# The seam between attention and experts: another order for the last period, earlier token splits, a one-step router sum, ScalarE scaling

## Chip, cores and metric

The kernel runs on one core of one Trainium2 chip. The metric is device time in microseconds; the median of the runs is compared. All times below are of one core.

## What is computed

Block-causal attention over 8 batches x 8 heads x 576 rows x 64 columns in float32 (a query block of 64 sees all key blocks up to its own). The heads are laid side by side into 4608 tokens of 512 numbers, which go through a two-level mixture of experts: a group softmax (4 groups) and an expert softmax inside the chosen group (4 experts), the best of each taken; then two layers of the one chosen expert, scaled by both weights.

```
scores = where(block_i >= block_j, q @ k.T / 8, -1e9)
x = softmax(scores) @ v                     # -> (4608, 512)
g = argmax(x @ w_group);  e = argmax(x @ w_expert[g])
out = p_g * p_e * (relu(x @ w1[g, e]) @ w2[g, e])
```

## The kernel before

The program is one list of instructions per engine, in an order that the kernel writes out by hand. Each engine works through its own list in order. TensorE, VectorE (DVE in the rows), ScalarE (ACT), GpSimd (POOL) and SyncE (SP, which issues most DMAs) are kept in step by semaphores.

**Attention.** 32 pairs of heads (4 pairs per batch) go through a software pipeline of periods. `ORDER` is the order of steps in one period: `S8@1` is the scores of row block 8 of the pair one period back, `D` the row maxima (VectorE), `E` the exponentials (ScalarE), `T` the transposes of the probabilities, `t` their evacuation to SBUF, `V` the values, `v` their evacuation, `K`, `k`, `j`, `h`, `l` the preparation of queries and keys. Four periods make a batch, and the router's steps of a finished batch ride in the same list: `R` reciprocals of the softmax sums, `X` transposes of the attention output to token rows, their scaling and their store to DRAM (`xd`), `L`/`n` router logits, `Y` their small transposes, `M` the sum of the logits over heads, `G0` and `G1` the two picks (group, expert), `G2` the prefix counts, `G4` the rank matmuls, `G3` the places, `Z` five scatters of token ids into the table `tab` (GpSimd). `LAST` names the router steps that are left over.

**PSUM.** During the attention one pool of four buffers of two banks rotates (`wide`). `experts()` closes it and opens the pools of the experts: `ps_h` (first layer), `ps_y` (two output banks), `ps_m0` and `ps_m1`. Some of the new tiles lie over buffers that must be read out first.

**Experts.** Slot "e" is the early expert: 512 tokens of the fullest expert over the first six batches, found by `early`, gathered (`xge`, four gathers of 128 rows) before the last two batches are done. So expert work can start while the last router results are still being made. The other slots run after `final` has made the row table (`rowi`) of all batches; their ids are read and their tokens gathered (`xg`). Weights arrive as `raw` pieces and are split into two float32r parts: `wh` by a ScalarE cast, `wl` by a VectorE subtraction (`piece`, two halves per unit); so are the tokens (`xt`) and the activations (`g1`: `hi` by ScalarE's relu, `lf` by VectorE). A unit `g1` (first layer) or `g2` (second) of slot "e" is 12 matmuls of 512 columns. `plan` writes the order of the units and a due time for each weight piece; `run` goes through it, and `hooks` hang the last batch's router steps behind units by number. In slot "e" the order was g1 0, g1 1, g2 0, g1 2, g2 1, and so on; `FREE` is the unit from which weights and gathers of the routed experts may be issued.

**The seam.** Order of issue before: the last period (scores, values of pair 30, transposes of pair 31), the left-over steps of batch 6, `R` of batch 7, two chunks of early tokens split (`xts`), the first weight pieces, the values of pair 31, the other two chunks, weights, unit g1 0, the logits `L` of batch 7, unit g1 1, `X0`, `Y`, `M`, `X1`, `X2`, the new PSUM pools, `G0`, `G1`, then the units with `G2`, `G4`, `G3`, `Z` and `final` behind units 2 to 4.

## Time and profile before

| what | value |
|---|---|
| median of 3 runs | 837.87 us (837.8 to 838.12) |
| profiled execution: time, span | 836.7 us, 835.0 us |
| mean granted TensorE clock | 0.991 |
| TensorE matmuls busy | 795.5 us (95%) |
| VectorE / ScalarE / GpSimd busy | 529.3 / 504.6 / 265.9 us |

A row of the timeline gives the start in microseconds from the span's start, the busy time of the group of like instructions, engine and line, what is written from what, the count, and in brackets how long the engine had been idle and what ended that. "issue" stands where the profile names no releaser. The granted clock is 1.00 at 2.4 GHz and 0.50 at 1.2 GHz.

### The profile page before, as it was taken

The page shows a single profiled execution, that of the slowest core. Times are in us where ns is not written, and L with a number is a line of the kernel's source. Part 1 is how long each engine was busy: PE and PEld are TensorE (multiplying, and loading weights), DVE is VectorE, ACT ScalarE, POOL GpSimd, SP SyncE. Part 2 cuts the span into 40 slices and gives each one's busy share as a digit, 9 for nine tenths or more (in the row PEclk, how much of TensorE's full clock was granted, in tenths as well). Part 3 has the DMA queues.
Part 4 walks back from the last instruction along what each step waited for, and adds up shares of the span by engine and source line. Part 5 has one row for each costly group of instructions (what it writes and reads, how often), then busy time and mean ns, then how long its engine had stood idle before and what let it go on. Part 6 is the DMA issues. An engine that isn't in the chain of part 4 may idle for free.

```text
span 835.0 us, 20289 instructions
## 1 busy us (share of the span) xinstructions
PE 795.5 (95%) x7649; PEld 649.7 (78%) x7649; DVE 529.3 (63%) x1102; ACT 504.6 (60%) x1273; POOL 265.9 (32%) x444
## 2 busy tenths in 40 slices
PE   8899999999999999879999999999999999999996
PEld 4677777777777777657888888888988989888885
DVE  4566989898989898668353544554444655655552
ACT  4899999999999998742342433433344445545541
POOL 3563344444444345443232211221221221131101
PEclk9899999999999999999999999999999999999999
DMA  7466473626363633641555736645544666575471
GB/s 153 114 185 181 109 157 78 155 71 150 83 152 78 145 84 90 198 153 36 177 166 162 236 117 205 201 133 192 197 145 148 203 207 191 179 237 177 151 236 39
DMA packets 182258, 126.67 MB, mean 152 GB/s; under 512 B 124902, under 2 KB 156214, under 8 KB 182160
## 3 DMA queue, kind: packets, MB, share of 16 engines
q1 hardware_dynamic: 173072, 100.73, 43.4%
q0 software_dynamic: 9088, 24.64, 8.6%
q8 instruction: 61, 1.00, 0.6%
q14 instruction: 37, 0.30, 0.1%
HBM read 100.88 MB, written 24.59 MB: 150 GB/s over the span
## 4 chain that ended last, share of the span: by engine, by line
PE 54%; DVE 1%; issue 0%; POOLq 0%; ACT 0%; ACTq 0%
PE y L1002 20%; PE h L957 19%; PE y L1007 5%; PE h L952 4%; PE ye L1002 2%; PE xp L925 2%; PE he L957 2%; POOLq L1293 0%; DVE gsc L712 0%; DVE gdd L710 0%; DVE goh L714 0%; DVE pre L742 0%; PE spill L612 0%; ACT ys L1024 0%; DVE sel L724 0%
## 5 line engine op out<-in xcount | busy, mean ns | idle before, releaser
L242 ACT ACTIVATE pb<-s,nm 128x512 f32<-128x512 f32 (+4 forms) x288 | 156.7, 556 | 31.3 <-DVE nm L230 26.7
L957 PE MATMUL h<-xt,wh 128*128 128x264 f32 (+6 forms) x704 | 155.3, 312 | 0.0
L909 DVE TENSOR_TENSOR wl<-raw,wh 128x512 fp32r<-128x512 f32 x192 | 123.4, 685 | 11.2 <-ACT wh L908 10.6
L230 DVE TENSOR_REDUCE nm<-s 128x2 f32<-128x1024 f32 (+4 forms) x160 | 122.9, 801 | 11.1 <-PE s L225 5.8
L957 PEld LDWEIGHTS h<-xt,wh 128*128 128x128 f32 x704 | 119.3, 188 | 9.1
L908 ACT CAST wh<-raw 128x512 fp32r<-128x512 f32 x192 | 108.8, 620 | 2.0 <-DMA raw<-in_moe_w_dram 1.7
L957 PE MATMUL h<-xt,wl 128*128 128x264 f32 (+6 forms) x352 | 109.3, 311 | 0.0
L1002 PE MATMUL y<-wh,hring 128*128 128x512 f32 x306 | 107.2, 401 | 0.0
L221 PE MATMUL s<-qk 64*128 64x512 f32 (+3 forms) x768 | 90.8, 351 | 12.6 <-ACT pb L242 7.3
L275 ACT COPY pt<-tp 128x1024 f32<-128x1024 f32 (+4 forms) x160 | 100.8, 747 | 0.5 <-PE tp L150 0.5
L1031 POOL DMA_INDIRECT out_dram<-ys,ids x40 | 41.2, 1029 | 183.4 <-DVE ys L1027 170.0
L970 ACT ACTIVATE hring<-h 128x288 fp32r<-128x288 f32 (+7 forms) x62 | 28.9, 466 | 114.0 <-PE h L957 55.3
L974 DVE SCALAR_TENSOR_TENSOR hring<-h,hring 128x32 fp32r<-128x32 f32 (+7 forms) x112 | 35.7, 357 | 97.5 <-ACT hring L970 89.2
L304 PE MATMUL o<-pt,vb 128*64 128x320 f32 (+4 forms) x896 | 93.9, 360 | 1.1 <-issue 1.1
L187 POOL CAST qk<-nf 128x640 fp32r<-128x640 f32 (+1 forms) x63 | 43.0, 694 | 150.8 <-ACT nf L275 140.4
L304 PEld LDWEIGHTS o<-pt,vb 128*64 128x64 f32 x896 | 59.6, 137 | 35.9 <-issue 5.1
L221 PEld LDWEIGHTS s<-qk 64*128 64x128 f32 x768 | 58.9, 190 | 24.8 <-issue 11.2
L872 POOL DMA_INDIRECT xg<-xd,ids x40 | 42.0, 1049 | 105.7 <-DMA ids<-tab 55.5
L150 PE MATMUL tp<-ident,pb 64*128 64x64 f32 x1600 | 65.5, 227 | 7.6 <-ACT pb L242 6.8
L150 PEld LDWEIGHTS tp<-ident,pb 64*128 64x128 f32 x1600 | 58.1, 141 | 14.3 <-ACT pb L242 8.0
L957 PEld LDWEIGHTS h<-xt,wl 128*128 128x128 f32 x352 | 66.2, 188 | 1.2
L1002 PEld LDWEIGHTS y<-wh,hring 128*128 128x128 f32 x306 | 57.6, 188 | 11.8
(236 smaller groups left out, 1396.5 us busy)
## 6 DMA issues: line engine op xcount, KB each, us to landing
raw<-in_moe_w_dram SPq DMA_DIRECT2D x96, 512.0 KB
natk<-in_k_dram SPq DMA_DIRECT2D x32, 256.0 KB
natq<-in_q_dram SPq DMA_DIRECT2D x32, 256.0 KB
vb<-in_v_dram SPq DMA_DIRECT2D x64, 128.0 KB
wh<-in_moe_w_dram SPq DMA_DIRECT2D x16, 512.0 KB
xd<-xns SPq DMA_DIRECT2D x14, 512.0 KB
tab<-fill POOLq DMA_DIRECT2D x10, 512.0 KB
rawe<-in_moe_w_dram SPq DMA_DIRECT2D x8, 512.0 KB
```

Source lines behind the costliest of these rows:

```text
L150: self.nc.tensor.transpose(out=out[:, z], in_=src[r], identity=self.c["ident"][r, r])
L187: (eng or self.side(("h", n))).tensor_copy(r["qk"][:, 0, o], r["nf"][:, o])
L221: nc.tensor.matmul(st[:, z, :], lhsT=t[p, hq, S + P * u:S + P * u + P], rhs=t[p, hk, 0:w], start=x == 0, stop=False)
L230: self.nc.vector.tensor_reduce(out=o, in_=r["s", u], op=ALU.max, axis=ax, negate=True)
L242: nc.scalar.activation(reg, src, AF.Exp, bias=r["nm"][:, t:t + 1], accum_out=self.sms[b][:, pr, z, u:u + 1])
L275: return self.nc.scalar.copy(dst, src)
L304: nc.tensor.matmul(o[64 * a:64 * a + 64, hf, c0:c0 + BLK * (b1 - t)], lhsT=r["v"][:, a, j, :], rhs=pt[:, PTJ * j + t:PTJ * j + b1, a, :], ...
L872: self.nc.gpsimd.indirect_dma_start(out=x[0:n], out_offset=None, in_=src, in_offset=bass.IndirectOffsetOnAxis(ap=s["ids"][0:n, c, 0:1], ax ...
L908: nc.scalar.copy(h[:, sl], s["raw", u][:, sl])
L909: nc.vector.tensor_tensor(out=l[:, sl], in0=s["raw", u][:, sl], in1=h[:, sl].bitcast(F32), op=ALU.subtract)
L957: nc.tensor.matmul(o, lhsT=ww[:, dc, f], rhs=rr[:, dc, t], start=dc == 0 and x == 0, stop=dc == 3 and x == 2)
L1002: nc.tensor.matmul(y[c][0:n], lhsT=hh, rhs=w, start=k == 0 and x == 0, stop=k == 7 and x == 2)
```

## The change

- The last period has its own order (`END`) outside the loop; all its evacuations are on ScalarE. `X0` of batch 6 moves into it; the token rows go to single row buffers instead of the attention's staging buffers.
- All four early chunks are transposed and split in pairs (`xt_pair`) ahead of the attention pools' closing and the last values. `R` of batch 7 moves behind the weights, and one pair of weight pieces behind the logits is no longer issued there. `G4`, `G3` and `Z` of batch 6 move behind unit g1 0 and the logits.
- In slot "e" g2 runs two units behind g1; the third unit's relu goes to a row buffer, and GpSimd makes `hi` from it. The new PSUM pools come in another order, one unit later. The hooks move one unit later; `FREE` is 8.
- The router's sum over heads is one reduction per part on VectorE; the addition on GpSimd goes.
- The last batch's `X` is done tile by tile (`tokens`): four 128-wide transposes, eight ScalarE activations with a scale per row, a store; behind units 3 to 7. Before, ScalarE copied and GpSimd multiplied.
- In periods 30 and 31 the hooks (batch 5's scatters and `early`; the early expert's index, ids, weights and gathers) come at closer steps: 3 and 1 instead of 7.

```diff
@@ -53,6 +53,10 @@
 Y1@4 X2@5 G3@6 E0@0 V@2 n1@3d E5@0 E1@0 E4@0 M1@4 j0@-1a h0@-1a G2@5 j1@-1a Y0@3 T1@1 T4@1 R0@2 X1@5 h1@-1a
 l1@-1a v@2a X0@6 L0@2 t1@1a T3@0 t4@1a n0@2a t3@0a M0@3 T2@1 t2@1a t0@1a G0@4 G1@4 l0@-1d S1@0 D1@0 E2@0
 E3@0
+""")
+
+END, END_DVE = parse("""
+S8@1 D8@1 E8@1 X2@5 G2@5 V@2 v@2a X1@5 T1@1 T4@1 T2@1 t1@1a t4@1a t2@1a t0@1a X0@5
 """)
 
 LAST = [("G", 0), ("G", 1), ("G", 2), ("G", 4), ("G", 3)] + [("X", j) for j in range(3)] + [("Z", j) for j in range(NT)]
@@ -101,8 +105,8 @@
         self.psx.close()
         tc, ctx = self.tc, self.ctx
         self.ps_h = ctx.enter_context(tc.tile_pool(name="ps_h", bufs=2, space=PSUM))
+        self.ps_m = [ctx.enter_context(tc.tile_pool(name=f"ps_m{i}", bufs=2, space=PSUM)) for i in range(2)]
         self.ps_y = ctx.enter_context(tc.tile_pool(name="ps_y", bufs=1, space=PSUM))
-        self.ps_m = [ctx.enter_context(tc.tile_pool(name=f"ps_m{i}", bufs=2, space=PSUM)) for i in range(2)]
 
     def clear(self):
         nc = self.nc
@@ -400,7 +404,7 @@
 DLEAD = 14000.0
 GLEAD = 24000.0
 ILEAD = 40000.0
-FREE = 7
+FREE = 8
 HK = 5
 
 
@@ -647,21 +651,19 @@
             for y in range(2):
                 nc.gpsimd.tensor_copy(ry[:, y].rearrange("p t (z c) -> p z t c", z=2), rx[:, :, :, 2 * y:2 * y + 2])
         elif k == "X":
+            if at.moe:
+                return self.tokens(at, b, (j,))
             q0, n, nt = 256 * j, TQN[2 * j], min(2, NTB - 2 * j)
             ps = at.wide(f"xn{b}_{j}")[:, :, 0:256 * nt].rearrange("p z (x d) -> p z x d", d=D)
             for t in range(nt):
                 for c in range(4):
                     at.flip(ps[0:n, :, 4 * t + c, :], xT[:, c, q0 + P * t:q0 + P * t + n])
-            last = b == NTOK // S - 1
-            for t0, m in [(t, 1) for t in range(nt)] if last else [(0, nt)]:
-                xn = (self.rows if last else at.nat).tile([P, m if last else 2, 512], F32, tag="row" if last else "xn", name=f"xns{b}_{j}_{t0}")[0:n, 0:m]
-                xv = xn.rearrange("p t (c z d) -> p z (t c) d", z=2, d=D)
-                eng, src = nc.vector, ps[0:n, :, 4 * t0:4 * (t0 + m), :]
-                if last:
-                    nc.scalar.copy(xv, src)
-                    eng, src = nc.gpsimd, xv
+            one = at.closed
+            for t0, m in [(t, 1) for t in range(nt)] if one else [(0, nt)]:
+                xn = (self.rows if one else at.nat).tile([P, m if one else 2, 512], F32, tag="row" if one else "xn", name=f"xns{b}_{j}_{t0}")[0:n, 0:m]
                 rv = st["rx"][0:n, :, 2 * j + t0:2 * j + t0 + m, :].rearrange("p z t c -> p z (t c)").unsqueeze(3)
-                eng.tensor_tensor(out=xv, in0=src, in1=rv.broadcast_to([n, 2, 4 * m, D]), op=ALU.mult)
+                nc.vector.tensor_tensor(out=xn.rearrange("p t (c z d) -> p z (t c) d", z=2, d=D), in0=ps[0:n, :, 4 * t0:4 * (t0 + m), :],
+                                        in1=rv.broadcast_to([n, 2, 4 * m, D]), op=ALU.mult)
                 r0 = b * S + q0 + P * t0
                 nc.sync.dma_start(self.xd[r0:r0 + n * m, :].rearrange("(t p) d -> p t d", t=m), xn)
         elif k == "L":
@@ -684,21 +686,31 @@
         elif k == "M":
             if j == 0:
                 st["lg"] = self.pool.tile([P, NTB, 20], F32, tag="lg", name=f"lgs{b}")
-                st["lp"] = self.pool.tile([P, 2, NTB, 20], F32, tag="lp", name=f"lps{b}")
             t0, nt = 4 * j, 4 - 3 * j
             tmp = self.pool.tile([P, 2, 16, 20], F32, tag="tmp", name=f"tmp{b}_{j}")
             src = st.pop(("ps", j))[:, :, 0:nt * 128].rearrange("p y (h j) -> p y h j", j=32)[:, :, :, 0:20]
             rv = st["ry"][:, :, t0:t0 + nt, :].rearrange("p y t h -> p y (t h)").unsqueeze(3)
             nc.vector.tensor_tensor(out=tmp[:, :, 0:4 * nt], in0=src, in1=rv.broadcast_to([P, 2, 4 * nt, 20]), op=ALU.mult)
-            for y in range(2):
-                nc.vector.tensor_reduce(out=st["lp"][:, y, t0:t0 + nt, :],
-                                        in_=tmp[:, y, 0:4 * nt].rearrange("p (t h) j -> p t j h", h=4), op=ALU.add, axis=AX.X)
-            if j == 1:
-                nc.gpsimd.tensor_tensor(out=st["lg"], in0=st["lp"][:, 0], in1=st["lp"][:, 1], op=ALU.add)
+            nc.vector.tensor_reduce(out=st["lg"][:, t0:t0 + nt, :], op=ALU.add, axis=AX.XY,
+                                    in_=tmp[:, :, 0:4 * nt].rearrange("p y (t h) j -> p t j y h", h=4))
         elif k == "Z":
             self.scatter(b, st, j)
         elif k == "G":
             getattr(self, f"phase{j}")(at, b, st)
+
+    def tokens(self, at, b, ts):
+        nc = self.nc
+        for t in ts:
+            n = TQN[t]
+            ps = at.psT(f"xn{b}_{t}")
+            for c in range(4):
+                nc.tensor.transpose(out=ps[0:n, P * c:P * c + P], in_=at.xTs[b][:, c, P * t:P * t + n], identity=self.c["ident"])
+            xn = self.rows.tile([P, 512], F32, tag="row", name=f"xns{b}_{t}")[0:n]
+            for c in range(4):
+                for z in range(2):
+                    o = slice(P * c + D * z, P * c + D * z + D)
+                    nc.scalar.activation(xn[:, o], ps[0:n, o], AF.Copy, scale=self.st[b]["rx"][0:n, z, t, c:c + 1])
+            nc.sync.dma_start(self.xd[b * S + P * t:b * S + P * t + n, :], xn)
 
     def pick(self, lg, nm, b):
         nc = self.nc
@@ -931,6 +944,21 @@
             return
         nc.scalar.copy(xh, pv)
         nc.vector.tensor_tensor(out=xl, in0=pv, in1=xh.bitcast(F32), op=ALU.subtract)
+
+    def xt_pair(self, s, c):
+        nc = self.nc
+        if c == 0:
+            s["xt"] = self.at.pt.tile([P, PTB], F32R, tag="pt", name=f"xt{s['n']}")
+            s["xh"], s["xl"] = [s["xt"][:, PTB // 2 * z:PTB // 2 * z + 2048].rearrange("p (d w) -> p d w", d=4) for z in range(2)]
+        ps = self.at.wide(f"xp{s['n']}_{c}")
+        for z in range(2):
+            for dc in range(4):
+                nc.tensor.transpose(out=ps[:, z, dc * P:dc * P + P], in_=s["x"][c + z][:, dc * P:(dc + 1) * P], identity=self.c["ident"])
+        src = ps.rearrange("p z (d w) -> p z d w", w=P)
+        xh, xl = [s[x][:, :, c * P:c * P + 2 * P].rearrange("p d (z w) -> p z d w", z=2) for x in ("xh", "xl")]
+        nc.scalar.copy(xh, src)
+        nc.vector.tensor_tensor(out=xl, in0=src, in1=xh.bitcast(F32), op=ALU.subtract)
+        self.nxt += 2
 
     def g1(self, s, b):
         nc = self.nc
@@ -952,6 +980,8 @@
                         nc.tensor.matmul(o, lhsT=w[0][:, dc, f].bitcast(F32), rhs=s["xh"][:, dc, t].bitcast(F32),
                                          start=dc == 0, stop=dc == 3)
                         continue
+                    if dc == 3 and s["n"] == "e" and b in self.mid:
+                        self.mid.pop(b)()
                     wh, wl = w
                     for x, (ww, rr) in enumerate(((wh, s["xh"]), (wh, s["xl"]), (wl, s["xh"]))):
                         nc.tensor.matmul(o, lhsT=ww[:, dc, f], rhs=rr[:, dc, t],
@@ -967,7 +997,13 @@
         for a, p in ps:
             wa = min(T, w0)
             pv = p.rearrange("p (k t) -> p k t", t=wa)
-            nc.scalar.activation(hi[:, :, a:a + wa], pv, AF.Relu)
+            if s["n"] == "e" and b == 2:
+                h = self.ro.rows.tile([P, 512], F32, tag="row", name="h2")
+                nc.scalar.activation(h, p, AF.Relu)
+                pv = h.rearrange("p (k t) -> p k t", t=wa)
+                nc.gpsimd.tensor_copy(hi, pv)
+            else:
+                nc.scalar.activation(hi[:, :, a:a + wa], pv, AF.Relu)
             for t, t0, t1 in ((lf, 0, F), (lt, F, T)):
                 q0, q1 = max(a, t0), min(a + wa, t1)
                 if q0 < q1:
@@ -1045,8 +1081,10 @@
                 if b == 0:
                     if prev is not None:
                         seq.append(prev)
-                else:
-                    seq.append((s, "g2", b - 1))
+                elif o or b > 1:
+                    seq.append((s, "g2", b - (1 if o else 2)))
+            if o == 0:
+                seq.append((s, "g2", s["nb"] - 2))
             prev = (s, "g2", s["nb"] - 1)
         seq.append(prev)
         self.seq = seq
@@ -1209,13 +1247,15 @@
         slots = [moe.slot("e", FULL, rowe, slice(0, 1))]
         slots += [moe.slot(i, CAPS[i], rowi, slice(i, i + 1)) for i in EXEC]
         moe.plan(slots)
-        for x in range(N + 1):
+        for x in range(N):
             hooks, step = (), 7
             if x == eb + 7:
+                step = 3
                 hooks = [lambda t=t: ro.token(at, EBAT - 1, t) for t in LAST if (EBAT - 1,) + t not in ro.done]
                 ear = ro.early(rowe)
                 hooks += [lambda: next(ear, None)] * 3
             if x == eb + 8:
+                step = 1
                 hooks = [lambda: moe.index(slots[0]), lambda: moe.getids(slots[0]),
                          lambda: moe.pump(False), lambda: moe.gathers(0, False)]
             if 1 <= x < 8:
@@ -1223,8 +1263,12 @@
                 for n in (1, 3) if x % 2 else (2,):
                     hooks[n] = lambda f=hooks[n]: (f(), next(fil, None))
             at.period(x, N, order, hooks, step)
-        for t in LAST:
-            ro.token(at, NBAT - 2, t)
+        at.on_dve, at.closed = END_DVE, True
+        at.load_v(N - 1)
+        for tok, lag in END:
+            at.token(N - lag, tok, N)
+        moe.xt_pair(slots[0], 0)
+        moe.xt_pair(slots[0], 2)
         inner.close()
         moe.open(ctx)
         last = NBAT - 1
@@ -1232,36 +1276,34 @@
         fin = ro.final(rowi, slots[1])
         step = lambda: next(fin, None)
         hooks = {
-            2: [lambda: b("G", 2)],
-            3: [lambda: b("G", 4), lambda: b("G", 3)] + [lambda j=j: b("Z", j) for j in range(NTB)],
-            4: [step, step, step, step],
-            5: [lambda: moe.getids(slots[1])],
+            3: [lambda: b("G", 2), lambda: b("X", 0)],
+            4: [lambda: b("G", 4), lambda: b("G", 3), lambda: b("X", 1)] + [lambda j=j: b("Z", j) for j in range(NTB)],
+            5: [lambda: b("X", 2), step, step, step, step],
+            6: [lambda: moe.getids(slots[1]), lambda: b("X", 3)],
+            7: [lambda: b("X", 4)],
         }
         spl = ro.spill(at, rowo, cnti)
         for n in range(60, 66):
             hooks[n] = [lambda: next(spl, None)]
         run = moe.run(hooks)
-        b("R", 0)
-        moe.xts(moe.begin[0], 2)
         moe.advance(2, 99)
         for tok, lag in order:
             if tok[0] in "tVvj" and lag == 2:
                 at.token(N - 1, tok, N)
-        moe.xts(moe.begin[0])
         moe.advance(2, 99)
         moe.grow()
+        b("R", 0)
         next(run)
         for j in range(2):
             b("L", j)
             b("n", j)
-        moe.advance(2, 99)
+        for t in LAST:
+            ro.token(at, last - 1, t)
         next(run)
-        b("X", 0)
         for j in range(2):
             b("Y", j)
             b("M", j)
-        for j in range(1, 3):
-            b("X", j)
+        next(run)
         at.experts()
         b("G", 0)
         b("G", 1)
```

## Rows read from the trace of the kernel before

**Rows 1.** Waits from 320 to 420: engine, line, releaser; us in total, times, longest.
```profile
DVE gmx L709 <- POOL lgs L697: 6.1, 2, 5.6
...
PE ye L1002 <- ACT xns L661: 1.4, 1, 1.4
```

**Rows 2.** Timeline of VectorE in the seam: start us, busy us, what, idle before it.
```profile
344.61 0.18 DVE L709 TENSOR_REDUCE gmx<-lgs 128x5 f32<-128x20 f32 x1 [5.58 <-POOL lgs L697]
...
347.11 0.18 DVE L714 TENSOR_TENSOR eoh<-esc,em 128x20 f32<-128x20 f32 x1
...
349.46 0.97 DVE L742 TENSOR_TENSOR pre<-pre,o 128x16 bf16<-128x16 bf16 x5
...
354.47 0.17 DVE L641 TENSOR_SCALAR sm<-sm 128x40 f32<-128x40 f32 x1
...
355.63 1.29 DVE L933 TENSOR_TENSOR xte<-xpe,xte 128x512 fp32r<-128x512 f32 x2
...
358.88 1.29 DVE L909 TENSOR_TENSOR wle<-rawe,whe 128x512 fp32r<-128x512 f32 x2 [1.96 <-issue]
...
371.21 0.81 DVE L692 TENSOR_TENSOR tmp<-ly,ry 128x640 f32<-128x640 f32 x1
...
372.06 1.29 DVE L694 TENSOR_REDUCE lps<-tmp 128x80 f32<-128x320 f32 x2
...
375.65 0.97 DVE L712 SCALAR_TENSOR_TENSOR gsc<-gdd,desc 128x20 f32<-128x20 f32 x1
```

**Rows 3.** Timeline of TensorE in the seam, the same columns.
```profile
343.97 2.93 PE L304 MATMUL o<-pt,vb 128*64 128x256 f32 x28 [0.49 <-issue]
...
349.00 0.46 PE L150 MATMUL tp<-ident,pb 64*128 64x64 f32 x8 [2.10 <-ACT pb L242]
...
352.49 1.09 PE L925 MATMUL xpe<-ident,xge 128*128 128x128 f32 x8 [0.42 <-DVE xns L664]
...
360.51 0.49 PE L957 MATMUL he<-xte,whe 128*128 128x512 f32 x1 [3.04 <-issue]
...
365.39 0.40 PE L957 MATMUL he<-xte,wle 128*128 128x512 f32 x1
...
403.82 0.66 PE L925 MATMUL xp<-ident,xg 128*128 128x128 f32 x4 [0.37 <-issue]
```

**Rows 4.** A window of 1 us: length, busy us of each engine, granted clock, DMA, GB/s.
```profile
363.00:364.00 1.00, 1.00 (x4) 0.81 (x3) 0.00 (x0) 0.00 (x0) 0.00 (x0) 0.50 0.35 77
```

**Rows 5.** Chain that ended last, from 330 to 420: start us, us, what.
```profile
380.92 2.90 PE ye L1002 x12
...
383.81 2.81 PE he L957 x12
```

**Rows 6.** Timelines of GpSimd and SyncE: as rows 2.
```profile
330.69 0.66 POOL L187 CAST qk<-nf 128x576 fp32r<-128x576 f32 x1 [4.40 <-DVE fin L521]
...
349.18 5.77 SPq L666 DMA_DIRECT2D xd<-xns  x3
...
371.28 2.04 POOL L664 TENSOR_TENSOR xns<-xns,rx 128x512 f32<-128x512 f32 x2 [10.59 <-ACT xns L661]
...
384.02 1.33 POOL L786 DMA_INDIRECT tab<-pay,pi  x1 [6.31 <-issue]
...
390.36 0.49 SPq L590 DMA_DIRECT2D rowi<-fin  x1
...
396.77 1.00 POOL L872 DMA_INDIRECT xg<-xd,ids  x1 [6.34 <-DMA ids<-tab]
```

**Rows 7.** Timeline of ScalarE: as rows 2.
```profile
330.40 0.22 ACT L275 COPY nf<-o 128x64 f32<-128x64 f32 x1
...
353.24 1.07 ACT L932 CAST xte<-xpe 128x512 fp32r<-128x512 f32 x2 [0.88 <-PE xpe L925]
...
403.49 0.60 ACT L970 ACTIVATE hring<-he 128x512 fp32r<-128x512 f32 x1 [3.99 <-issue]
```

**Rows 8.** Waits from 60 to 320: as rows 1.
```profile
DVE gmx L709 <- POOL lgs L697: 3.1, 6, 0.5
```

3 lines of the change are left out of this document (2 added, 1 removed).

## Prediction

> **What bounds the kernel now.** I read the 40 slices of the page first: TensorE is nearly full before slice 16 and after slice 19, and thinner between. The seam from the attention to the experts, 340 to 381 us, is the only stretch with much to win. There I read windows of 1 us, then the timeline engine by engine, then the chain of waits. The reader is to see four losses.
>
> First, VectorE sits idle for 5.58 us until GpSimd has added the two halves of the router's logits [rows 1, 2]. GpSimd reaches that addition only after four gathers, since its queue runs in order. The scores' row maxima stand behind it on VectorE, so the exponentials and the transposes of the last pair come late: TensorE waits 2.10 us at 349.00 [rows 3]. Second, TensorE waits 3.04 us before the first expert matmul at 360.51 [rows 3]: half of the early tokens are split only behind the last values, and the first weight residual starts at 358.88 after an unexplained idle of 1.96 us [rows 2]. Third, after that hole the granted clock is 0.50, the lower level of 1.2 GHz, in the window from 363 [rows 4]. The first unit runs from 360.51 to 365.79 [rows 3], 5.3 us, where a later one takes 2.81 [rows 5]: 2.5 lost, to the clock and to late residuals. Fourth, TensorE waits 1.4 us for PSUM before the first second-layer unit [rows 1].
>
> The chain of waits says what follows: it enters by the router's VectorE steps and leaves through the rank matmuls into TensorE at 380.92 [rows 5]; from there TensorE is the bound to the end.
>
> **The change, up to the first expert matmul.** The addition on GpSimd goes, so the wait of 5.58 goes. The values of pair 30 still start at 343.97 (ScalarE's evacuation ahead of them does not move) and end at 346.90. Behind them on TensorE stand now the 16-matmul token transposes X1, three groups of transposes T1, T4, T2, X0, the four expert chunks, and the last values. T1's 8 transposes take 0.46 [rows 3], so T4's 10 take some 0.5 and the 16 of X1, T2 and X0 some 0.7 each; a pair of chunks takes 1.09 and the values 2.93, as those of pair 30 [rows 3]. Sum 0.7 + 0.5 + 0.5 + 0.7 + 0.7 + 2.2 + 2.9 = 8.1 to 8.2: **355.0**. Are the operands there? In the old order T1 starts 1.7 behind the end of the picks (347.29 [rows 2] to 349.00); in the new one the picks end near 342, ScalarE is free at 343.9, and T1's turn is at 347.6. The transposes of the chunks end at 351.0 and 352.1; two splits of 1.07 on ScalarE [rows 7] and a weight piece like them end by 354.4. Two residuals take VectorE 1.29 [rows 2]: it has those of the tokens at 354.8 and that of the weights at 356.1, when the unit has reached its second half. The first expert matmul starts at **355.0 instead of 360.5: 5.5 us**.
>
> The wait of 1.96 before the weight residual I put on the token store: the new weight buffers lie over the old staging buffer, whose third store is issued only around 354.6 (SyncE's row ends at 354.95) [rows 6]. Batch 6 now uses the row buffers, which stay. If it is something else, 358.9 stays the start of that residual and the gain falls by about 3.
>
> With no hole the clock should stay at its upper level, so the first unit takes 3.0.
>
> **The order behind it.** Two more things decide when the rank matmuls run: TensorE's arrival and VectorE's chain. TensorE: 355.0, five units of 2.81, 0.2 of start, logits 1.15, the older batch's rank matmuls 0.3, the small logit transposes 0.8, one token tile 0.55, and some 0.7 because the third unit's PSUM comes free only when ScalarE has read it: **372.7**. VectorE, in its order from 356.1: weight residual 1.3 (its cast ends the wait: 357.7), router reciprocals 1.15 (354.47 to 355.63 in [rows 2]), residual of unit 0 0.7, weights 1.3, five small steps of the older batch at 0.2, a wait for unit 1 to 363.15, 0.7, weights 1.3, the two logit sums 2.9, a wait, 0.7, weights 1.3, the two picks 2.7 (344.61 to 347.29 [rows 2]), and the prefix 1.3 (0.3 ahead of the five steps of 0.97 in [rows 2]). The sums: products 0.85 [rows 2] and 0.35, plus one reduction of 640 numbers in place of two of 320, which cost 1.29 together [rows 2]; I take 1.25, and 0.4 for the small one. Bounds of the large reduction: 0.65 (one row of 320) and 1.3.
>
> The second wait in that list is new. The third unit's activation goes through GpSimd's copy, and GpSimd's queue then holds the older batch's five scatters, moved here. They take 1.28 us each (384.02 to 390.43, where GpSimd's idle time ahead of 396.77 begins [rows 6]) and begin at 362.0, so the copy ends at 369.0; VectorE is there at 368.1 and waits 1.0. Behind it stand the picks, and behind these the rank matmuls: **375.1**. TensorE waits 2.4.
>
> The picks cost 2.7 and not what they cost in the last batch, where single steps on 20 numbers took up to 0.97 against 0.18 [rows 2], while GpSimd multiplied token rows [rows 6]; that multiply now goes to ScalarE. The Trainium skill (SBUF — State Buffer, SBUF: two separate sides) calls this port an exclusive lock that a VectorE instruction with two SBUF inputs and a GpSimd instruction hold in turn, each for its whole length; the long steps agree. By that rule GpSimd's new copy, 0.6 as an estimate from its 0.66 for 576 columns [rows 6], could hold VectorE once more: 375.7.
>
> Sum up to the end of the rank matmuls: before, 380.92 with four units done; after, 375.5 with five. 5.4 plus one unit of 2.8, less the four token tiles still to come, 4 x 0.55 = 2.2 (each is four chunk transposes, half the row of 1.09): **6.0 us**. If the rank matmuls waited for nothing it would be 8.4.
>
> **Costed at nothing.** Token scaling on ScalarE: eight steps of 64 columns at 0.22 [rows 7], 1.8 per tile, 9 in all against 2.9 of copies; later in the slot ScalarE waits 3.99 us in a row [rows 7], and each tile stands a unit apart. Without that cover each tile would cost 1.8. Batch 5's scatters earlier: the fifth moves ahead of a cast before which GpSimd is idle for 4.40 [rows 6]; uncovered it is 1.3. The earlier bookkeeping of the early expert: about 2 us of VectorE work moves into a busy part of its period; 0 to 1, I take 0. The first weights are asked for some 7 us sooner, and their space is free. The weight gate of 8 instead of 7 sits on SyncE and GpSimd, behind the row table that is waited for anyway: at most one unit, 2.8, if the gathers were not later.
>
> **The gathers of the first routed expert.** The row table is written 9.4 after the rank matmuls before (390.36) and by my order about 8.1 after them: 383.6. The first gather follows 6.4 later, at 390.0 (396.77 before) [rows 6], or at 390.6, when the last token tile has landed, since its store now stands on SyncE behind the row read. The transposes of the data started 7.0 behind that (403.82, after a wait of 0.37 [rows 3]), so 397.6. TensorE gets there after the 11th unit behind the first at 397.4. Wait 0.2, about as before.
>
> **The attention.** In six earlier batches VectorE waits 0.51 each for the same addition, 3.1 in all [rows 8], and saves 0.14 per batch in the sums. How much of it is on the path, no row says. Bounds 0 and 3.9; I take **1.0**, nearer the lower end, because the row maxima of only one period in four stand right behind it.
>
> Total 7.0. The profiled execution had a span of 835.0 and a time of 836.7; it would become 828.0 and 829.7. The median shown is 1.17 above it, so I forecast **830.9**, with its own range 829 to 833.
>
> **Rivals.** (A) No wait at the rank matmuls, because VectorE is quicker than my list: 2.4 more, 828.5, or 827 with more of the attention's 3.9. For it: the reduction may cost 0.65, and weights may be split earlier. Against it: the list is mostly rows. Chance 0.20 for below 829. (B) Part of the hole stays: the residual's wait is not the store (3 less), or the wait of 2.4 at the rank matmuls lowers the clock again (up to 2.5 less); 833 to 836.2. For it: the clock fell behind 3.04 idle [rows 3, 4]. Against it: 2.4 is shorter. Chance 0.22. (C) No gain that shows, the seam's savings all given back at the gathers: within 0.2%, 0.05. (D) Slower, one mechanism: the store of the last token tile, behind SyncE's row read, holds back the gathers. Each microsecond beyond 397.4 costs one; it decides when the first gather starts after about 399 (7.0 plus 1.7 beyond 390.4), and two more late give 841. For it: the queue order is new. Against it: from the row table to the first gather all took only 6.4 [rows 6]. Chance 0.08. My forecast has 0.45. About 0.2%, 1.7 us, is what a measurement here can tell from no change.
>
> That the change does not do what it says is in B: the early tokens are split ahead, but the start waits all the same.
>
> The range: 827.0 leaves out about 0.06 of A; 835.6 leaves out D, C and a little of B, 0.14. Faster 0.87, same 0.05, slower 0.08.
>
> **What would show it.** Right: the first expert matmul 5 to 6 us earlier, its unit near 3 us at a clock of 1.00; no long wait of VectorE for the logits; a wait of 1 to 3 us ahead of the last batch's rank matmuls, with VectorE full; single pick steps near 0.18. Wrong: a hole still ahead of that first matmul, half clock behind it, a wait over 4 us at the rank matmuls, or expert transposes that wait several microseconds for gathered rows.

## The result, and the profile after

The changed kernel took 826.41 us (median of 4 runs, 825.2 to 827.3) where the kernel before took 838.0 on the same chip: ratio 0.9856, 95% interval 0.9837 to 0.9876. The prediction was 830.9 with a range of 827.0 to 835.6, so the sign was right and the time is 0.6 below the range. The profiled execution took 827.03 with a span of 825.1; before it was 836.7 and 835.0.

Where the 9.83 us of span went can be read from a few starts on TensorE's timeline: the first values matmul of pairs 0, 28, 29 and 30 (V0 ... V30), and the first matmul of the first routed expert (h). The stretches add up, and the same columns serve for every run below. "sum": two steps or one; "book": bookkeeping at every 7th step or early; "order": of the seam, old or new; "wait": of VectorE's `gmx` for the logits of the second-last batch.

```
kernel    sum      book  order  wait    V0   V0-28  28-29  29-30  V30-h  h-end
before    two      7th   old    5.6   32.80  292.3  11.8   7.0    70.6   420.4
after     one      early new    0     30.27  289.8  13.9   7.2    63.7   420.3
difference                            -2.5   -2.6   +2.0   +0.2   -6.9   -0.1
```

The changed stretches are V0 to V28 (the sum in six batches) and V30 to h (the seam): 9.4 less together. The other 0.3 is the start, 2.5 less, against periods 30 and 31, 2.3 more; the start turns out below to go with the granted clock, and period 30 mostly with the chip.

TensorE's timeline after, in the seam [rows 3 for before]:

```profile
341.15 2.93 PE L308 MATMUL o<-pt,vb 128*64 128x256 f32 x28 [0.48 <-ACT pt L279]
344.00 0.71 PE L154 MATMUL xn<-ident,xT 64*128 64x64 f32 x16
...
346.29 1.97 PE L956 MATMUL xpe<-ident,xge 128*128 128x128 f32 x16
348.19 2.92 PE L308 MATMUL o<-pt,vb 128*64 128x256 f32 x28
351.05 0.74 PE L987 MATMUL he<-xte,whe 128*128 128x512 f32 x2
...
363.55 0.47 PE L1038 MATMUL ye<-whe,hring 128*128 128x512 f32 x1 [1.16 <-ACT h L1002]
...
370.20 0.20 PE L774 MATMUL rk<-o,tri 128*128 128x80 bf16 x1 [0.36 <-DVE o L751]
371.00 0.20 PE L775 MATMUL rk<-pre,ones 128*128 128x80 bf16 x1 [0.60 <-DVE pre L754]
...
394.13 0.63 PE L938 MATMUL xp<-ident,xg 128*128 128x128 f32 x4 [1.31 <-DMA xg<-xd,ids]
...
404.88 0.41 PE L987 MATMUL h<-xt,wh 128*128 128x264 f32 x2
```

Read downwards: the hole ahead of the first expert matmul is gone (9.90 from pair 30's values to it, 16.54 before). Behind it stand waits of 1.16 ahead of the first second-layer unit, for ScalarE's activation of the third unit, of 0.36 and 0.60 at the rank matmuls, and of 1.31 for gathered rows.

VectorE after [rows 2]:

```profile
335.33 0.43 DVE L694 TENSOR_REDUCE lgs<-tmp 128x20 f32<-128x160 f32 x1
335.79 0.18 DVE L721 TENSOR_REDUCE gmx<-lgs 128x5 f32<-128x20 f32 x1
...
361.94 1.23 DVE L694 TENSOR_REDUCE lgs<-tmp 128x80 f32<-128x640 f32 x1
...
365.25 0.69 DVE L1010 SCALAR_TENSOR_TENSOR hx<-h,hx 128x512 fp32r<-128x512 f32 x1 [1.37 <-issue]
...
367.06 0.17 DVE L721 TENSOR_REDUCE gmx<-lgs 128x5 f32<-128x20 f32 x1
...
369.56 0.18 DVE L726 TENSOR_TENSOR eoh<-esc,em 128x20 f32<-128x20 f32 x1
...
370.18 0.97 DVE L754 TENSOR_TENSOR pre<-pre,o 128x16 bf16<-128x16 bf16 x5
```

The row maximum `gmx` now follows the sum with no idle bracket. The single large reduction takes 1.23, against 1.29 for the two it replaces. The third unit's residual at 365.25 waits 1.37; the profile names no releaser, but GpSimd's copy, which it reads, ends at 365.21. The picks take 2.7, each step at its short price.

The clock, one window as [rows 4]: the upper level (2.4 GHz) is granted in the first unit, which runs from 351.05 to 354.1.

```profile
353.00:354.00 1.00, 1.00 (x5) 0.56 (x3) 0.97 (x4) 0.00 (x0) 0.00 (x0) 1.00 0.62 162
```

SyncE's queue and GpSimd's after [rows 6]:

```profile
379.48 0.52 SPq L594 DMA_DIRECT2D rowi<-fin  x1
383.17 1.71 SPq L874 DMA_DIRECT2D ids<-tab  x3
384.98 0.94 SPq L713 DMA_DIRECT2D xd<-xns  x2
```

```profile
364.59 0.62 POOL L1004 CAST hx<-h 128x512 fp32r<-128x512 f32 x1
...
388.46 1.00 POOL L885 DMA_INDIRECT xg<-xd,ids  x1 [7.74 <-DMA xd<-xns]
```

The last two token stores stand behind the row table and the indices, as the prediction's rival D said, and the first gather waits for them: it follows the table by 9.0, where I took 6.4.

### The profile page after: what moved, and what is told of

Same layout as the page of the kernel before. It is cut to its first block, busy times and chain, and to the rows that moved or that the text cites. A ratio compares the mean times of both kernels' runs of the same rounds, so it can differ in the third digit from the quotient of the medians.

```text
span 825.1 us, 20267 instructions
## 1 busy us (share of the span) xinstructions
PE 791.1 (96%) x7629; PEld 647.5 (78%) x7629; DVE 527.2 (64%) x1085; ACT 510.7 (62%) x1307; POOL 258.8 (31%) x432
## 4 chain that ended last, share of the span: by engine, by line
PE 72%; DVE 13%; ACT 9%; issue 2%; DMA 1%; POOL 1%; another core or an unknown queue 1%; POOLq 0%; SPq 0%; DVEq 0%; ACTq 0%
PE y L1038 20%; PE h L987 19%; PE o L308 8%; ACT pb L246 6%; PE y L1043 5%; PE h L980 4%; PE s L225 4%; DVE nm L234 4%; DVE qk L196 4%; ACT pt L279 2%; PE xp L938 2%; PE tp L154 2%; DVE xns L665 2%; PE he L987 2%; PE ye L1038 2%
## 5 line engine op out<-in xcount | busy, mean ns | idle before, releaser
L922 DVE TENSOR_TENSOR wl<-raw,wh 128x512 fp32r<-128x512 f32 x192 | 123.4, 685 | 11.3 <-ACT wh L921 10.8
L225 PE MATMUL s<-qk 64*128 64x512 f32 (+3 forms) x768 | 88.7, 348 | 10.6 <-ACT pb L246 8.7
L1038 PEld LDWEIGHTS y<-wh,hring 128*128 128x128 f32 x306 | 57.5, 188 | 11.8
L154 PEld LDWEIGHTS tp<-ident,pb 64*128 64x128 f32 x1600 | 57.3, 139 | 10.9 <-ACT pb L246 4.7
```

Of the source, the lines that this page charges most:

```text
L154: self.nc.tensor.transpose(out=out[:, z], in_=src[r], identity=self.c["ident"][r, r])
L225: nc.tensor.matmul(st[:, z, :], lhsT=t[p, hq, S + P * u:S + P * u + P], rhs=t[p, hk, 0:w], start=x == 0, stop=False)
L922: nc.vector.tensor_tensor(out=l[:, sl], in0=s["raw", u][:, sl], in1=h[:, sl].bitcast(F32), op=ALU.subtract)
L1038: nc.tensor.matmul(y[c][0:n], lhsT=hh, rhs=w, start=k == 0 and x == 0, stop=k == 7 and x == 2)
```

## Experiments

**Controls.** Kernel before, twice, and the changed kernel once more, all unchanged, on other chips.

> The kernel before, unchanged, as a control. Theory (the 2.5 us by which the changed kernel is ahead at the first values matmul, 30.27 against 32.80, before any changed instruction has run, is the granted clock of 20 to 35 us in one execution, 0.84/0.50/0.91 against 1.00): the first values matmul of this execution stands near 30.3 if the clock of that stretch is granted in full and near 32.8 if it is not, the median stays within 0.2% of 838, and the profiled time goes with the start. Rival (the start is the change's, by another placement of its code or tiles): 32.8 again, whatever the clock.

> The kernel before, unchanged, again. On three chips it took 838.0, 836.3 and 831.9 to 832.2 us, and the change was worth 11.6 on the first and 8.6 on the last. Theory (the chips differ by the 2 us of period 30, which the last one does not show, and by the start): on a chip that gives 832 to 833, period 30 is 9.7 and the first values matmul near 30, and the stretch from pair 30 to the first routed expert is 70 to 72.5 as on the others. Rival (the seam of the kernel before is itself different there, so that the sum has less to win): 66 to 69.

> The changed kernel, unchanged, as a control beside the next three on the same chip. Theory (the 2 us by which period 30 is longer, 11.8 between the values of pairs 28 and 29 against 9.7, goes with the chip or the execution and not with the edits, since one chip showed 9.7 for four kernels of both orders and two others 11.7 to 13.9 for all the rest): this kernel's period 30 equals that of the other three here, within 0.6. Rival (the earlier bookkeeping costs 0.5 to 2 there): longer here than in the kernel with the bookkeeping at every seventh step by that much. From pair 30 to the first routed expert 63.7 to 64.4.

```
kernel    sum      book  order  wait    V0   V0-28  28-29  29-30  V30-h   median  before on that chip
c_before  two      7th   old    6.2   30.72  292.2  11.8   7.1    72.5    836.4   836.3
c_bef2    two      7th   old    5.8   30.48  292.3   9.8   7.0    70.8    831.3   831.9
a_ctl     one      early new    0     29.52  289.8   9.7   6.8    63.7    823.6   832.2
```

The changed stretches repeat: attention 292.2 to 292.3 against 289.8, seam 70.6 to 72.5 against 63.7. V0 and period 30 do not go with the order of the seam. V0 goes with the clock granted in 25 to 30 us; the same window in two executions of the kernel before and of a variant of the changed one:

```profile
25.00:30.00 5.00, 4.63 (x60) 4.43 (x61) 2.62 (x3) 4.62 (x14) 3.77 (x4) 0.50 0.23 55
```

```profile
25.00:30.00 5.00, 4.55 (x76) 3.95 (x76) 3.49 (x5) 5.00 (x15) 3.78 (x4) 1.00 0.44 99
```

```profile
25.00:30.00 5.00, 4.46 (x59) 4.26 (x60) 2.62 (x3) 4.63 (x13) 3.77 (x4) 0.50 0.23 52
```

The first is the profile of before (V0 at 32.80), the second c_before (30.72), the third u_h2 below (32.94). The theory on the start holds. Period 30 took 9.7 to 9.8 in eleven profiles of either order and 11.7 to 13.9 in the other six, and a_ctl, the changed kernel itself, has 9.7, as its theory and that of c_bef2 said. Of the six long ones the four with the bookkeeping at every seventh step have 11.7 to 11.8, the two with early bookkeeping 12.4 and 13.9. Since the chips differ, a time that an expectation names is compared below by its distance from the kernel before or after that stood behind it (838 and 826.4). The changed kernel gained 8.6 here (ratio 0.9903, 0.9875 to 0.9931) and 11.6 first; its two stretches say 9.4.

**The sum alone, and the same with VectorE doing the addition.** On the kernel before:

```
s_sum:  nc.vector.tensor_reduce(out=st["lg"][:, t0:t0 + nt, :], op=ALU.add, axis=AX.XY, ...)   # as in the change
s_dve: -nc.gpsimd.tensor_tensor(out=st["lg"], in0=st["lp"][:, 0], in1=st["lp"][:, 1], op=ALU.add)
       +nc.vector.tensor_tensor(out=st["lg"], in0=st["lp"][:, 0], in1=st["lp"][:, 1], op=ALU.add)
```

> The kernel before with nothing changed but the router sum: one reduction over both columns and heads where there were two reductions and an addition by GpSimd. Theory (the sum is worth 0.43 us a batch on the path of the attention, as the steps in the lead of the changed kernel say, and in the last batch the VectorE chain to the rank matmuls is shorter by some 3): lead over the kernel before of 2.6 at pair 28 beyond the start, and 831 to 833 in all. Rival (as I predicted: 1.0 in the attention; the lead's steps come from other parts): lead of 1.0 and 833 to 835. Second rival (TensorE is what the rank matmuls wait for in the kernel before): the lead of the attention alone, 835 or more.

> The kernel before with one word changed: the addition of the two halves of the logits runs on VectorE, behind its two reductions, and not on GpSimd. Theory (what the one-step sum removes is the wait for GpSimd, 0.5 us in each batch and 5.6 to 6.2 at the seam; the shape of the reduction counts for little): lead in the attention of 0.25 to 0.35 a batch, 1.5 to 2 in all at pair 28, the wait at the seam gone, 828 to 830. Rival (the single reduction itself is what gains): within 0.3% of the kernel before, 834 to 838.

```
kernel    sum      book  order  wait    V0   V0-28  28-29  29-30  V30-h   median  before on that chip
s_sum     one      7th   old    0     31.70  289.6  11.7   7.1    66.2    827.4   836.3  ratio 0.9875 (0.9855 to 0.9894)
s_dve     VectorE  7th   old    0     30.32  289.9   9.8   7.0    65.8    825.0   831.9  ratio 0.9911 (0.9892 to 0.9929)
```

A surprise in size: the sum alone gains 8.9 (2.6 in the attention and 6.3 at the seam against c_before on the same chip), where I expected 5 to 7. The theory held for the attention. s_dve gains 6.9, less than the 8 to 10 expected and far from its rival's zero; in the attention it gains 2.4 where 1.5 to 2 were expected. So it is the wait that counts and not the reduction, as s_dve's VectorE timeline shows: two reductions and the addition on one engine, and no idle ahead of `gmx`.

```profile
331.62 0.49 DVE L694 TENSOR_REDUCE lps<-tmp 128x20 f32<-128x80 f32 x2
332.14 0.26 DVE L697 TENSOR_TENSOR lgs<-lps 128x100 f32<-128x100 f32 x1
332.44 0.17 DVE L709 TENSOR_REDUCE gmx<-lgs 128x5 f32<-128x20 f32 x1
```

In the kernel before (c_before), GpSimd's timeline shows why it waited: the addition stands behind the last of four gathers.

```profile
341.46 1.00 POOL L872 DMA_INDIRECT xge<-xd,idse  x1 [0.27 <-POOL xge L871]
342.49 0.40 POOL L697 TENSOR_TENSOR lgs<-lps 128x100 f32<-128x100 f32 x1
```

In the attention the whole gain lies in one period of four, that of the picks: from one pair's first values to the next it takes 10.7 in c_bef2 and 10.3 in s_dve and s_sum, and the other three periods take the same in all. It is not the wait's 0.51 itself that is won. VectorE starts the picks 0.2 earlier in s_dve and 0.5 earlier in s_sum, and both gain 0.41 to 0.44 a batch. What the picks run into is GpSimd's multiply for the next scores, here in the sixth batch of c_bef2, VectorE and then GpSimd:

```profile
293.42 0.17 DVE L709 TENSOR_REDUCE gmx<-lgs 128x5 f32<-128x20 f32 x1 [0.51 <-POOL lgs L697]
...
295.90 1.52 DVE L712 SCALAR_TENSOR_TENSOR esc<-edd,desc 128x20 f32<-128x20 f32 x1
...
297.66 0.19 DVE L714 TENSOR_TENSOR eoh<-esc,em 128x20 f32<-128x20 f32 x1
```

```profile
295.83 1.55 POOL L192 TENSOR_TENSOR qk<-nf,qk 128x640 fp32r<-128x640 f32 x1
```

and in s_dve:

```profile
294.05 1.21 DVE L714 TENSOR_TENSOR eoh<-esc,em 128x20 f32<-128x20 f32 x1
```

```profile
293.65 1.57 POOL L192 TENSOR_TENSOR qk<-nf,qk 128x640 fp32r<-128x640 f32 x1
```

In both the step that meets the multiply ends 0.04 behind it. In c_bef2 that leaves two steps to go, 0.43; in s_dve, and in s_sum with 1.39, it is the last step. By these rows the two steps are the gain: the row maximum behind the picks, ScalarE and TensorE come that much earlier. No run moves the multiply itself.

**The change without the sum, and the bookkeeping.** Three runs put the two-step sum back, on either order, with either bookkeeping; u_hooks takes the early bookkeeping from the changed kernel.

```
u_sum:   changed kernel, sum in two reductions and GpSimd's addition as before
u_sumhk: u_sum, and without  step = 3 / step = 1  in the two last hooked periods
s_hooks: kernel before, with  step = 3 / step = 1  there
u_hooks: changed kernel, without them
```

> The changed kernel with the router sum in two reductions and GpSimd's addition again; all else of the change stays. Theory (the sum's wait for GpSimd's in-order queue is the main cost at the seam, and the new order alone does little): VectorE's row maximum behind the sum of the second-last batch waits again for the logits, some 3 us, since GpSimd's four gathers end at 338.1 and VectorE is ready at 335.8; the attention loses 2.6; from the first values matmul to pair 30 and on to the experts 3 more; 831.5 to 833.5. Rival (order and sum each close most of the seam's hole by themselves): the attention's 2.6 alone, 828.5 to 829.5. Second rival (the sum is everything): 835.5 to 837.

> The changed kernel with the sum in two reductions and GpSimd's addition again, and the bookkeeping back at every seventh step; order, early tokens and ScalarE's scaling stay. Theory (with the two-step sum alone VectorE waited 2.8 for the logits, since the earlier bookkeeping had brought the gathers forward; without it GpSimd reaches the addition 2.5 to 3.5 later): VectorE's wait 5 to 6.5, from pair 30 to the first routed expert 67 to 69 against 64.9, 2 to 4 more than with the two-step sum alone. Rival (the new order at the seam no longer needs these logits early): 64.9 again.

> The kernel before with nothing changed but the bookkeeping of the second-last and third-last periods at every third and every step, as in the changed kernel. Theory (the long wait at the seam comes from GpSimd reaching the addition only behind its four gathers; with the gathers some 3 us earlier the wait falls from 5.6 to 6.2 to about 3, and the seam follows): from pair 30 to the first routed expert 66.5 to 69 instead of 70.6 to 72.5, the attention as before, 2 to 4 less in all. Rival (the wait does not move, since the indices land no earlier): within 0.3% of the kernel before. Second rival (the earlier bookkeeping itself costs in period 30): 0.5 to 2 more.

> The changed kernel with the bookkeeping of the second-last and third-last periods back at every seventh step (the changed kernel has every third and every step). Theory (the five scatters in a row at 316 to 322 and the work behind them hold a semaphore of TensorE or its queue for 2 us in period 30: the lead falls from 5.08 to 3.05 there): the stall of VectorE's row maximum falls from 4.15 to about 2.6 and the time by 2, to 824.5, if the token gathers still come in time. Rival A (the stall has nothing to do with the hooks): the lead falls as before and the time is 826.4. Rival B (the later bookkeeping makes the gathers of the first four chunks late, which the changed kernel needs earlier): a wait of TensorE at the first chunk, time 827 to 830.

```
kernel    sum      book  order  wait    V0   V0-28  28-29  29-30  V30-h   median  before on that chip
u_sum     two      early new    2.8   31.49  292.4   9.7   6.8    64.9    827.7   831.9  ratio 0.9946 (0.9927 to 0.9966)
u_sumhk   two      7th   new    5.2   30.16  292.2   9.8   7.0    67.8    829.2   831.9  ratio 0.9969 (0.9949 to 0.9988)
s_hooks   two      early old    2.8   29.39  292.4   9.7   6.8    67.3    828.2   831.9  ratio 0.9965 (0.9945 to 0.9986)
u_hooks   one      7th   new    0     31.43  289.8  11.8   7.1    64.4    824.5   836.3  ratio 0.9864 (0.9843 to 0.9884)
```

VectorE's timelines show the wait that these share (u_sumhk, then s_hooks):

```profile
339.44 0.18 DVE L725 TENSOR_REDUCE gmx<-lgs 128x5 f32<-128x20 f32 x1 [5.20 <-POOL lgs L699]
```

```profile
336.17 0.18 DVE L709 TENSOR_REDUCE gmx<-lgs 128x5 f32<-128x20 f32 x1 [2.79 <-POOL lgs L697]
```

With these the seam comes apart: the new order adds to the rest, while the sum and the bookkeeping overlap, since both shorten the same wait. The new order is worth 1.8 to 3.0 at any wait (70.8 to 67.8, 67.3 to 64.9, 66.2 to 64.4). Early bookkeeping is worth 2.9 to 3.5 while the addition is on GpSimd, because the gathers end sooner and the wait falls from between 5.2 and 5.8 to 2.8; with the one-step sum it is worth 0.7 at most. The sum is worth 4.4 to 6.3 in the old order with late gathers, 3.4 in the new with late ones and 1.2 in the new with early ones. The expectations of s_hooks and, by the stretches, of u_sumhk held; u_sum lies between its theory (5 to 7 more than the changed kernel) and its rival (2 to 3): 3.8 by the stretches, since the wait of 2.8 cost only 1.2 at the seam; its second rival, that the sum is everything, falls. u_hooks has VectorE's stall in period 30 at 2.6 and the period at 11.8, the sizes that its theory named, but so have c_before and s_sum on the same chip (2.5, 11.7 to 11.8), and its gain of 11.8 is that of the changed kernel (11.6). u_pairs below, on that chip with early bookkeeping, has 12.4. So where period 30 is long a price of the early bookkeeping, 0.6 to 2.1 by one profile each, stays open; where it is short there is none (9.7 with it, 9.8 without).

**The early tokens in two halves.** On the changed kernel:

```
-moe.xt_pair(slots[0], 0); moe.xt_pair(slots[0], 2)      # ahead of the last values
+moe.xts(moe.begin[0], 2) ... moe.xts(moe.begin[0])      # two chunks before, two behind, as in the kernel before
```

> The changed kernel with the early token chunks of the first expert split as before: two behind the last tokens' weight work, two behind the last values, instead of all four ahead of the last values. Theory (the order at the seam is what closes the hole behind the last values; some 5 us with the half clock that follows it): from the last full values matmul to the first expert matmul 13 to 15 us instead of 9.9, and 829 to 831.5. Rival (the transposes are needed anyway and TensorE is busy either way): within 1 us of the changed kernel, 826 to 827.4.

Seam 64.9 against 63.7, median 827.8, ratio 0.9902 (0.9882 to 0.9921). From pair 30's values to the first expert matmul it takes 10.8, not 13 to 15. By the stretch the split ahead is worth 1.2, not 5; the medians, whose gain of 8.5 stands beside the change's 8.6 and 11.6, do not settle it. TensorE's timeline with the two halves back shows only 0.73 and 0.34 of hole:

```profile
350.04 0.49 PE L987 MATMUL he<-xte,whe 128*128 128x512 f32 x1 [0.73 <-ACT xte L945]
350.88 0.50 PE L987 MATMUL he<-xte,whe 128*128 128x512 f32 x1 [0.34 <-DVE xte L946]
```

So most of the hole of 3.04 [rows 3] did not come from the split's place. Nor did it come from the late logits: s_sum, in the old order but with no wait for them, still shows it, in two parts.

```profile
352.25 0.50 PE L953 MATMUL he<-xte,whe 128*128 128x512 f32 x1 [1.73 <-issue]
354.21 0.79 PE L953 MATMUL he<-xte,whe 128*128 128x512 f32 x1 [1.47 <-issue]
```

From the first values matmul of pair 31 to the end of the first expert unit all six profiles of the old order take 11.6 to 13.4, whether VectorE's wait was 5.6 to 6.2, 2.8 or 0; u_pairs takes 8.3 and the others of the new order 5.9 to 6.0. What the removed wait shortens lies ahead of that: from pair 30's values to pair 31's, 9.5 to 10.9 in the kernel before, 6.5 in s_sum and s_dve. So the hole was closed by the new order, and mostly by something in it other than the split's place; no run shows which part. At the first routed expert 1.8 to 3.0 of it are left, as above.

**ScalarE's scaling.** On the changed kernel:

```
-nc.scalar.activation(xn[:, o], ps[0:n, o], AF.Copy, scale=...)   # eight per tile
+nc.scalar.copy(xn, ps[0:n])
+nc.gpsimd.tensor_tensor(out=xv, in0=xv, in1=rv.broadcast_to([n, 2, 4, D]), op=ALU.mult)
```

> The changed kernel with the last batch's token rows copied by ScalarE and scaled by GpSimd, as before, instead of scaled by ScalarE alone. Theory (GpSimd's multiplies of token rows run while VectorE picks, and stretch single steps from 0.18 up to 0.97, so the rank matmuls come 2 us later and TensorE waits so much longer there): picks of 3.5 to 4.7 in all against 2.7, 827.5 to 828.5. Rival A (the tiles now stand a unit apart and do not fall on the picks): 826.4. Rival B (fewer ScalarE steps help): 825.5 to 826.

Seam 66.6 against 63.7 (64.3 for x_ids on the same chip); median 825.95, ratio 0.9931 (0.9909 to 0.9954). The loss at the seam, 2.9 (2.3 beside x_ids), is above the theory's 1.1 to 2.1, and comes by other steps than it named. GpSimd's and VectorE's timelines:

```profile
365.30 1.04 POOL L712 TENSOR_TENSOR xns<-xns,rx 128x512 f32<-128x512 f32 x1 [4.62 <-ACT xns L709]
368.57 1.04 POOL L712 TENSOR_TENSOR xns<-xns,rx 128x512 f32<-128x512 f32 x1 [2.24 <-ACT xns L709]
...
377.40 2.06 POOL L712 TENSOR_TENSOR xns<-xns,rx 128x512 f32<-128x512 f32 x2
```

```profile
364.94 0.18 DVE L726 TENSOR_TENSOR eoh<-esc,em 128x20 f32<-128x20 f32 x1
...
365.55 1.61 DVE L754 TENSOR_TENSOR pre<-pre,o 128x16 bf16<-128x16 bf16 x5
...
368.87 0.84 DVE L790 TENSOR_TENSOR t<-t,o 128x80 f32<-128x80 f32 x1
...
377.72 3.75 DVE L922 TENSOR_TENSOR wle<-rawe,whe 128x512 fp32r<-128x512 f32 x2
```

The picks end before the first multiply and stay short. The steps that do overlap one are stretched: 1.61 against 0.97, 0.84 against 0.23, 3.75 against 1.29. And the third multiply stands behind five scatters, so that SyncE, which waits to store its row, reads the row table only at 378.91, 2.9 behind the end of VectorE's last step for it. The Trainium skill (SBUF — State Buffer, SBUF: two separate sides) states an exclusive lock of the port that VectorE and GpSimd share, held for a whole instruction; these durations agree: the step at 368.87 ends at 369.71, 0.1 behind the multiply. In the changed kernel VectorE was idle while GpSimd copied, so that what I had worked out from this rule for the copy could not show.

**The waits that are left.** On the changed kernel:

```
x_ids:  -6: [lambda: moe.getids(slots[1]), lambda: b("X", 3)],  7: [lambda: b("X", 4)],
        +6: [lambda: b("X", 3)],  7: [lambda: b("X", 4), lambda: moe.getids(slots[1])],
x_act:  -nc.sync.dma_start(self.xd[...], xn)   +nc.scalar.dma_start(self.xd[...], xn)
x_acthk: x_act and the bookkeeping at every seventh step
u_h2:    third unit by nc.scalar.activation(hi[...], pv, AF.Relu) alone, without GpSimd's copy
```

> The changed kernel with the row table's read and the indices of the first routed expert asked for behind the last token tile, one unit later, so that on SyncE the last two tiles' stores stand ahead of the row read and not behind it. Theory (the gathers wait for these stores, 7.74 us behind the write of the table, and the transposes of the data 1.3 behind that): first gather 0.8 to 1.3 earlier behind the row table, TensorE's wait ahead of the first routed expert's transposes gone, 1.0 to 1.2 less, 825.2 to 825.4. Rival (the index steps on VectorE, now a unit later in its order, take as much as the stores gave): 826.4, or up to 1 more.

> The changed kernel with the last batch's token rows stored from ScalarE's own queue, right behind the step that writes them, and no longer from SyncE's, where the row table's read and the indices' loads stand ahead of the last two. Theory (the first routed gathers wait for these two stores, 7.0 to 7.7 us behind their queue, and with the stores earlier they would wait only for the indices, which land some 2 behind their issue): first gather 7.3 to 7.8 behind the row table instead of 9.0, TensorE's wait ahead of the first routed transposes (1.3 to 2.0) down to 0 to 0.6, 1.0 to 1.5 less than the control. Rival (the indices land no sooner than the stores do now): no change, within 0.4 of the control. Second rival (the issue of a store takes time of ScalarE, which here also frees the PSUM of the units): 0.5 to 1 more.

> Both: token rows stored from ScalarE's queue, and the bookkeeping of the two last periods at every seventh step. Theory (the place of that bookkeeping costs nothing that shows): equal to the stores alone, within 0.4. Rival (it costs 0.5 to 2 in period 30): that much less than with the stores alone. Second rival (later gathers of the early tokens hold the first four chunks back): more than with the stores alone.

> The changed kernel with the third unit of the early expert through ScalarE's activation alone, as the other units, without the copy by GpSimd behind the older batch's scatters. Theory (the copy ends 1.1 behind the last step of the sum, VectorE stands idle 1.37 for it and everything behind, the picks and the rank matmuls, is that much later; TensorE's wait of 1.0 there goes): 0.6 to 1.0 less than the control. Rival (without the copy ScalarE must wait until the first unit's place in the ring comes free, with the second layer now two units late, and the third unit's PSUM with it): TensorE waits 1 to 3 us ahead of the fourth or fifth unit, 1 to 2.5 more.

```
kernel    V30-h   median  before on that chip
x_ids     64.3    822.3   831.9   ratio 0.9883 (0.9862 to 0.9903)
x_act     63.9    821.8   832.2   ratio 0.9874 (0.9847 to 0.9902)
x_acthk   63.1    822.7   832.2   ratio 0.9892 (0.9867 to 0.9916)
u_h2      63.8    824.9   832.2   ratio 0.9909 (0.9885 to 0.9933)
a_ctl     63.7    823.6   832.2   ratio 0.9903 (0.9875 to 0.9931)
```

None differs from the control by more than the intervals. x_ids: the indices were asked for 6.5 behind the row table instead of 3.7, and the gather waited for them in place of the stores, 9.2 behind the table; its theory fails. x_act: the gather came 7.4 behind the row table, as expected, but its rows took longer; TensorE's timeline still shows the wait:

```profile
388.86 0.63 PE L938 MATMUL xp<-ident,xg 128*128 128x128 f32 x4 [1.51 <-DMA xg<-xd,ids]
```

From the gather's issue to these transposes it took 7.3, against 6.1 in a_ctl and 6.4 in x_acthk. x_acthk has the wait of 0.60 that was expected of x_act, and the shortest seam, 63.1, but its median is 0.9 above x_act's with overlapping intervals, so its theory (within 0.4) is not decided. Why the rows took longer, and whether x_act beats the changed kernel, stays open: 821.8 against 823.6, with overlapping intervals. u_h2: the waits at the rank matmuls go, but TensorE waits 2.1 instead of 1.2 ahead of the first second-layer unit and 1.8 for the gathers; nothing is won or lost. No version run here is shown to beat the changed kernel.

## Why the prediction was right in sign and 4.5 us too slow

- **The attention: the step that failed.** "How much of it is on the path, no row says. Bounds 0 and 3.9; I take 1.0": it was 2.6. All of s_sum, s_dve and the changed kernel have it (289.6 to 289.9), every kernel with GpSimd's addition has 292.2 to 292.4. My reason for the low end, that a row maximum stands right behind the picks in one period in four only, took off what was never there: the wait, too, comes once in four periods, and in just that period the row maximum and TensorE behind it come 0.41 to 0.44 earlier. That 2.6 lies near the wait's 3.1 [rows 8] is in part chance, since two steps behind GpSimd's multiply set it and not the wait's length.
- **The first expert matmul: 6.6 instead of 5.5.** Stretch by stretch I summed busy times of separate rows, 11.0 from pair 30's values to it; they overlap, and it took 9.9. The term was mis-sized, the mechanism right. That the store was the cause of the residual's wait of 1.96 was not tested: the wait stands, at 1.6 to 2.0, in all six profiles of the old order, and not in u_pairs, which has the new row buffers. That fits, but no run changes the buffers alone.
- **What was credited to what.** I had both the removed wait and the order for the 5.5 and could not part them. The runs do: the wait alone is worth 4.4 to 6.3 in the old order, the order 1.8 to 3.0, and the early tokens' two halves, to which I had put part of the hole, 1.2. The hole itself stays in s_sum and s_dve: the order closed it, and the removed wait shortened the stretch ahead of it.
- **From there to the rank matmuls: 20.3 against 20.5.** Terms off in both directions: the wait there 1.0 instead of 2.4, since TensorE came later; VectorE's list came out within 0.2, with the wait for GpSimd's copy at 1.4 instead of 1.0. The picks were short, as said; the multiplies that had stretched the last batch's picks before are not those of the row in [rows 6], which end at 373.32, but the next ones, from 374.54 to 377.58. The row table followed 8.1 behind, as said.
- **The gathers: 9.0 behind the row table instead of 6.4.** Rival D's mechanism is there at 1.1 of price, since TensorE then waits 1.3 where I had 0.2. By x_ids and x_act, moving the stores does not clearly win it back.
- **Costed at nothing:** early bookkeeping was right where period 30 is short (0.7 at most at the seam, as a gain) and stays open where it is long; ScalarE's scaling was right, and what it avoids, 2.3 to 2.9, I had not priced.
- **Chance.** Start and period 30 gave -2.5 and +2.0 in the profiled pair, which hid each other; whether all of the 2.0 is chance stays open, as said of the bookkeeping. By the two stretches the change is worth 9.4; I had 7.0. Of the 2.4 between, 1.6 are the attention and 0.9 the seam. The other 2.1 of the 4.5 are no step of mine: 0.3 from start and periods 30 and 31, 1.2 that I added because the median of before lay above its profile, and 0.6 by which the median after lies below its own.

## What to carry to other kernels

A small step that one engine hands to another and waits back for comes back only behind what stands ahead of it on the other engine's queue: here 0.4 us of addition kept VectorE waiting 0.5 in each batch and 5.6 behind four gathers, and the same addition on the waiting engine itself (0.26) gained some three quarters of what the change gained (2.4 and 4.8 of 9.4 by the stretches). What such a wait is worth is not its length: 0.5 came to 0.4, 5.6 to 6.2 came to 4.4 to 6.3, 2.8 to 1.2. Read what the waiting engine runs into next, and do not put the wait near nothing without a row that shows slack behind it. And when two parts of a change attack one stretch, expect their gains to overlap (8.9 and 4.2 alone, 8.6 to 11.6 together). Compare stretches between fixed events, not whole spans: chance at the start was here as large as a whole term.

## What was not expected of the hardware

- The clock granted in 25 to 30 us is 0.50, 0.66 to 0.71 or 1.00 in like kernels, with no edit that could set it, and the first values matmul then starts at 32.8 to 32.9, 31.3 to 31.7 or 29.3 to 30.7.
- Period 30 takes 9.7 or about 11.8 us (12.4 and 13.9 with early bookkeeping) with the same code. In the long ones VectorE's row maximum waits for a semaphore that the profile can't place, here c_before's waits of VectorE:

```profile
DVE nm L230 <- remote: 2.5, 1, 2.5
```

Pair 28's 28 values matmuls then spread over 3.5 to 4.8 from first to last start instead of 2.7. The profiles of three chips all show 9.7 to 9.8 and the four of another 11.7 to 12.4, with kernels of either order on two of the three and on the other; what decides it stays open.
- From the issue of the first routed gather to the transposes of its rows it took 5.7 to 7.3, unpredicted by anything that these runs vary.
